# A scheduled S4D-convolution and MLP kernel: where two 64-row matmuls stand among the convolution's steps, and the settings of its order

## The chip, the cores and the metric

The kernel runs on one core of a Trainium2 chip. The metric is the device time of one execution in microseconds (us). The kernel before takes 1095.59 us (median of three runs, 1095.1 to 1095.95).

The engines are named as the profile names them: PE (TensorE, matmuls), PEld (its weight loads), DVE (VectorE), ACT (ScalarE), POOL (GpSimd) and SP (SyncE, which issues most of the DMAs).

## The reference

The output is x + s * g for 2048 tokens of 576 channels. s is a state-space convolution along the tokens (S4D: a kernel made from complex exponentials, applied by FFT), and g is a gated MLP on each token:

```python
x = A_u
xn = _layernorm(x)
s = _A_ref(xn, log_A_real, A_imag, C_real, C_imag, log_dt, D_skip)   # FFT convolution, + u * D_skip
# _B_ref: y = layernorm(xn); h = gelu(y @ w1 + b1); h @ w2 + b2      (w1: 576x4608, w2: 4608x576)
g = _silu(_B_ref(xn, w1, b1, w2, b2))
return x + s * g
```

## The kernel before, in words

**The MLP sets the frame.** The 2048 tokens go in four blocks of 512 and the 4608 hidden channels in 12 groups of 384 (three chunks of 128), which gives 48 *slots* (`NSLOT`). A slot has 11 *positions* (`NPOS`): three of layer 1 (`layer1`, line 633, tiles mxa and mxb in PSUM) and eight of layer 2 (`layer2`, line 707). Every operand is split into a high and a low part, so a product takes three matmuls. In layer 1 a chunk takes 14 matmuls of 128 rows by 512 columns: 12 for the first 512 channels, and for the last 64 channels one on `w1r` with XR (64 rows of high and 64 rows of low parts together) and one more on `w1s`. Layer 2 takes 72 matmuls of 288 columns in a slot. Behind a layer-1 chunk stand a Gelu (ACT, line 671), a copy to the high part `hh` (ACT, 674) and a subtraction for the low part `hl` (DVE, 677); behind each fourth of layer 2 stands an addition to `acc` (DVE, 717).

**The pair.** `pair` (line 616) does the `w1s` work of two chunks, 0 and 2, by two matmuls of 64 rows each, one on array rows 0 to 63 and one on rows 64 to 127, side by side. Then neither chunk needs its `w1s` matmul, and takes 13 instead of 14 (`BEGUN` holds the chunks). The second one reads a copy of XR's upper half, which `load_pair` brings to partitions 64 to 127 in a tile that the program calls bias.

**The convolution** is done in six chunks of 96 channels. Each is a row of steps on PE, between ACT and DVE work: two x1 (array tile 64x128), two k1 (32x128), four s2 (64x32), two inv (32x64), one i1 (128x64), and the tables of the kernel (kg, 128x32, 36 in all). A kg may *ride* inside another step (`ride`, `lead`); inside an x1 it stands behind the x1's matmuls, inside the others ahead of them. All steps take their PSUM from two banks-of-two named cv, which DVE or ACT must empty before the next step but one.

**The order is planned when the program is built.** The class `Order` keeps a clock for each engine. PE's list is the frame of slots; `pe_turns` is asked behind certain positions whether a step of the convolution goes in there. It takes a step if its inputs are ready by the plan's clocks by some margin, if the pace (`EDGE`) allows it, and for a kg if ALONE and DUE allow it. X1, S2, INV, I1 and KG are the plan's durations of the steps, `LEN` those of the positions. The other engines' work is put in where the plan finds room; of steps that are ready together the line of `od.line()` that stands first goes first; HOLD puts single steps one or two places later than planned. Each engine then runs its list in that order. `pe_turns` sets a pair ahead of the first convolution step at a slot's edge (position 10), if its weights and its copy are there.

Of the kernel before, what the change touches and what calls it, by code (L numbers as in the profile page):

```python
# [18 lines left out]
P = 128  # L19
# [13 lines left out]
G = 3  # L33
# [18 lines left out]
class Order:  # L52
# [44 lines left out]
    def take(self, eng, dur, ready, tbl=None):  # L97
        start = max(self.t[eng], ready)
        if eng == "DVE" and self.shared and start < self.t["POOL"] - 0.4:
            dur *= 1.1  # L100
        if tbl and tbl != self.tbl:
            dur += 1.28
            self.tbl = tbl
        self.t[eng] = start + dur
        return start + dur + self.LAT
# [119 lines left out]
def mixer_kernel(ctx, tc, u, log_a_real, a_imag, c_real, c_imag, log_dt, d_skip, w1, b1, w2, b2,  # L225
                 f1, f2, g2, g1, tvals, ident, out, parts=("mlp", "s4d")):
    nc = tc.nc
# [6 lines left out]
    def bank2(name):  # L234
        return ps.tile([P, 2, TB], F32, name=name, bufs=2 if name == "cv" else 1)
# [236 lines left out]
    XR = sb.tile([P, 2, TB], F32R, name="XR")  # L472
    XQ = {}
# [58 lines left out]
    W = {}  # L532
# [56 lines left out]
    HID, LAST, Q1, Q2, IDM = {}, {}, {}, {}, []  # L589
    turn = [0]  # L590

    def mx(i):
        return "mxa" if (turn[0] + i) % 2 == 0 else "mxb"

    BEGUN = set()
# [10 lines left out]
            XQ[0] = sb.tile([P, D], F32R, name="bias2")[:, :TB]  # L606
        nc.sync.dma_start(XQ[0][64:].bitcast(F32), XR[:64, tb].bitcast(F32))

    def pair(tb):

        Q1[0] = bank2(mx(1))
        for e, x in enumerate((XR[:64, tb], XQ[0][64:])):
            r, k = slice(64 * e, 64 * e + 64), e * (G - 1)
            nc.tensor.matmul(Q1[0][:, e], W[1][3][r, k * P:(k + 1) * P], x, start=True, stop=False,  # L616
                             skip_group_check=True)
        BEGUN.update((0, G - 1))

    def layer1(g, tb, i):  # L620
        h, lo, r1, r2 = W[1]
# [331 lines left out]
    def tables(b):  # L953
# [37 lines left out]
        def weigh(part):  # L991
# [10 lines left out]
            else:  # L1002
# [7 lines left out]
                 step("DVE", dve(SB * NV), f(phase, 0), need=[("kg", b - 2)] if b > 1 else []),  # L1010
                 step("DVE", dve(n), f(phase, 1), hold=HOLD.get(("phase", b), 0)), step("ACT", act(SB * NV), whole),
                 step("DVE", dve(SB * NV), frac, hold=HOLD.get(("frac", b), 0)), step("ACT", act(SB * NV), fold, mark=("fold", b))],
                [step("ACT", act(SB * NV), f(sin, 0), need=[("fold", b)], mark=("sin", b, 0), tbl="sin"),
# [3 lines left out]
                + [step("DVE", dve((2, 2, 1, 1)[part] * n), f(weigh, part), need=[("sin", b, 1)],  # L1017
                        mark=("wu", b) if part == 3 else None, hold=HOLD.get(("weigh", b, part), 0)) for part in range(4)])

# [33 lines left out]
    def ride(host):  # L1053

        if not kl["steps"] or kl["steps"][0]["eng"] != "PE" or host["mark"][0] == "inv":
            return
        st, out = kl["steps"][:2]
        need = st["need"]
        if any(m not in od.marks for m in need) or max([kl["ready"]] + [od.marks[m] for m in need]) > od.t["PE"] - 0.4:
            return  # L1060
        del kl["steps"][:2]
        GUEST.append(st["fn"])
        host["dur"] += KG

        def behind():
            end = od.t["PE"] + od.LAT
            od.marks[st["mark"]] = kl["ready"] = end
            od.urgent.append((end, [dict(out, cv=0)]))
        return behind


    X1, S2, INV, I1, KG = 1.5, 1.75, 2.15, 3.05, 1.03

    HOLD = {("weigh", 19, 3): 1, ("phase", 19): 1, ("frac", 18): 2, ("k", 2, 1): (2, 1), (2, 0, 24): 1, (2, 1, 24): 1, ("k1", 2, 1, 2): 1}

    def chunk(c):

# [66 lines left out]
        def x1(i):  # L1144
# [18 lines left out]
            for d0 in (0, 24):  # L1163
                c0 = 48 * i + d0
                add("DVE", 0.9, lambda d0=d0, c0=c0: nc.vector.transpose(
                    A2[:, :, 0, c0:c0 + 24].rearrange("p k d r -> p d k r"), Q[d0]), cv=-1, hold=HOLD.get((c, i, d0), 0))

# [150 lines left out]
    NPOS = G + 8  # L1318
    NSLOT = 4 * NG
    od = Order(tc, nc)  # L1320
    od.pinned = True
    el, wl2, wl, nl2, pl, pl2, nl, ml, ml2, xl, wx, c3, c2, c1, c4, kl, tl, sl, vl, gl, odl, fl = [od.line() for _ in range(22)]
    nlh, mlh, mlt = od.line(), od.line(), od.line()
    od.lines = od.lines[-3:] + od.lines[:-3]

# [76 lines left out]


    L1 = 14 * 0.2315
    LEN = [L1] * G + [3 * n * 0.132 + 0.02 for n in (4, 2, 2, 4, 3, 3, 3, 3)]

    T0 = 12.5
    for e, t in dict(PE=0.0, ACT=4.6, DVE=3.7, POOL=3.8, SP=0.0).items():
# [98 lines left out]
    def wmark(n, which):  # L1507

        per = KB + 1 + G
        a = n * per + (0 if which == 1 else KB + 1)  # L1510
        return [("w", k) for k in range(a, a + (KB + 1 if which == 1 else G))]
# [67 lines left out]


    EDGE = 0.2, 0.6
    ALONE, DUE = 20.0, (160.0, 950.0)

    def pe_turns(limit=1, any_time=False, all_lines=True, edge=None):
        for x in (nl, pl, ml) + ((c3, c1, kl) if all_lines else ()):
            n = 0
            while n < (2 if x in (c1, nl) else limit):
                h = od.head(x)
                if h is None or h[0]["eng"] != "PE" or h[1] > od.t["PE"] + (0.3 if x is nl else -0.4):
                    break  # L1590
                if x is c1:
                    now = od.t["PE"]
                    gap = (END - now) / max(pace["left"], 1)
                    if n == 0 and pace["started"] and now < pace["last"] + EDGE[edge is None] * gap and not any_time:
                        break
                    pace["started"], pace["last"] = True, now
                    pace["left"] -= 1
                if x is kl and pace["started"]:
                    b = kl["steps"][0]["mark"][1]
                    wait = ("wu", b + 1) not in od.marks or od.t["PE"] < DUE[0] + b * (DUE[1] - DUE[0]) / NB  # L1600
                    if b < NB - 1 and od.t["PE"] < h[1] + (ALONE if wait else 3.0):
                        break
                if edge is not None and not BEGUN and x in (c3, c1, kl):
                    m = wmark(edge // 2, 1) + [("xq", edge)]
                    if all(k in od.marks and od.marks[k] < od.t["PE"] - 0.3 for k in m):
                        od.unit(lambda: pair(edge % 2), 0.24)
                behind = ride(h[0]) if x in (c1, c3) else None
                od.run(x)
                if behind:
                    behind()  # L1610
                od.pin()
                od.advance(od.t["PE"])
                n += 1

    LATER = {}

    def later(slot, pos, f):
# [53 lines left out]
    for slot in range(NSLOT):  # L1671
        turn[0] = slot + 1
        od.shared = slot > 1
        g, tb = slot // 2 % NG, slot % 2
        n = slot // 2
        final = slot >= NSLOT - 2
        for pos in range(NPOS):
            if pos < G:
# [9 lines left out]
                if pos == 2:  # L1688
                    BEGUN.clear()
                    k = slot % (2 * NG)  # L1690
# [16 lines left out]
            else:  # L1707
# [13 lines left out]
                if halves:  # L1721
                    dh = terms[0][1]
                    od.marks["z", dh] = od.t["PE"] + od.LAT
                    x = od.line()
# [3 lines left out]
                if split:  # L1728
                    add = cell[0]
                    for d in range(2) if j == 0 else (terms[0][1],):  # L1730
                        m = ("acc", slot, j, d)
# [3 lines left out]
                        x = od.line()  # L1735
# [3 lines left out]
                if last and not halves:  # L1739
# [4 lines left out]
                    elif final:  # L1744
                        x = el if slot < NSLOT - 1 else od.line()
# [3 lines left out]
                    elif g == NG - 1:  # L1749
                        for d in range(2):  # L1750
                            one, two = gate_store(4 * tb + j, d)
# [6 lines left out]
            for f in LATER.get((slot, pos), ()):  # L1758
                f()
            od.advance(od.t["PE"])  # L1760
            pe_turns(edge=slot + 1 if pos == NPOS - 1 else None, all_lines=pos in (0, 1, 2, G + 1, G + 3, G + 5, NPOS - 1))
    od.force(lambda: not od.urgent and not any(x["steps"] for x in od.lines))


# [52 lines left out]
```

## Time and profile before

| | us |
|---|---|
| median of three runs | 1095.59 |
| the profiled execution | 1095.67 |
| its span, first to last instruction | 1093.9 |
| PE busy | 1087.1 (99%) |
| DVE busy | 891.9 (82%) |
| ACT busy | 727.1 (66%) |
| POOL busy | 188.4 (17%) |

Matmuls are pipelined: a matmul of 288 columns is shown as 0.29 us long, and the next one starts 0.13 us behind it. What a matmul costs is therefore read from one start to the next, not from its duration. A row of the timeline merges instructions of one line and name that follow one another: start, time to the end of the last one, engine, line, what is written and read, shapes, and their count. The rows with "64\*128" are array tiles of 64 rows and 128 columns.

### The profile page before, as it was taken

To read this page: it belongs to the slowest core of one execution; us is meant where nothing else is said; L and a number is where in the kernel's file an instruction comes from. 1 tells how busy PE (TensorE), PEld (TensorE's weight loads), DVE (VectorE), ACT (ScalarE), POOL (GpSimd) and SP (SyncE) were. 2 spreads that over 40 slices of the span, in tenths; PEclk is the share of its full clock that TensorE was granted. 3 is DMA by queue.
4 is the path that set the end of the run, shared out by engine and by line. 5 is a ranking of instruction groups with operands and counts; after the bars stand their busy time and mean duration, and the time that the engine had idled before them with its cause. 6 is when DMAs were issued, how large, how long until landed. Compare 5 with 4: busy or idle time off the path is not lost.

```text
span 1093.9 us, 27052 instructions
## 1 busy us (share of the span) xinstructions
PE 1087.1 (99%) x11445; PEld 954.0 (87%) x11445; DVE 891.9 (82%) x1302; ACT 727.1 (66%) x1113; POOL 188.4 (17%) x261
## 2 busy tenths in 40 slices
PE   9999999999999999999999999999999999999998
PEld 7989899899888898888988888888888888888897
DVE  7798667889998879889899987997969888766367
ACT  6585699778676674767767848685675757534333
POOL 4566210153020100001100000000001021101132
PEclk9999999999999999999999999999999999999999
DMA  8746764626354152355624215143142434454444
GB/s 242 225 149 152 236 235 143 179 80 157 116 160 134 44 112 67 96 110 148 161 48 118 78 56 141 34 122 87 56 126 42 144 101 132 114 170 150 137 151 103
DMA packets 139553, 138.22 MB, mean 126 GB/s; under 512 B 88952, under 2 KB 105016, under 8 KB 138856
## 3 DMA queue, kind: packets, MB, share of 16 engines
q1 hardware_dynamic: 124424, 85.05, 29.0%
q0 software_dynamic: 14528, 50.71, 14.7%
q8 instruction: 89, 1.46, 0.6%
q10 hardware_dynamic: 480, 0.74, 0.3%
q14 instruction: 32, 0.26, 0.1%
HBM read 102.17 MB, written 36.63 MB: 127 GB/s over the span
## 4 chain that ended last, share of the span: by engine, by line
PE 95%; DVE 3%; ACT 1%; SPq 1%; issue 0%; DMA 0%; POOL 0%; DVEq 0%; ACTq 0%; POOLq 0%
PE mxb L707 20%; PE mxa L707 20%; PE mxa L633 20%; PE mxb L633 20%; PE cv L1217 3%; PE cv L1042 3%; PE cv L1260 2%; PE cv L1286 2%; PE cv L1188 1%; PE cv L1157 1%; PE mxa L1348 1%; DVE acc L717 0%; PE mxa L648 0%; SPq L1089 0%; PE mxb L616 0%
## 5 line engine op out<-in xcount | busy, mean ns | idle before, releaser
L677 DVE TENSOR_TENSOR hl<-h,hh 128x512 fp32r<-128x512 f32 x144 | 98.5, 687 | 99.2 <-ACT hh L674 98.4
L707 PE MATMUL mxa<-w2h,hh 128*128 128x288 f32 x573 | 170.3, 297 | 0.0
L707 PE MATMUL mxb<-w2h,hh 128*128 128x288 f32 x573 | 170.2, 297 | 0.0
L707 PE MATMUL mxb<-w2h,hl 128*128 128x288 f32 x573 | 169.3, 295 | 0.1
L707 PE MATMUL mxa<-w2h,hl 128*128 128x288 f32 x573 | 169.1, 295 | 0.0
L707 PE MATMUL mxa<-w2l,hh 128*128 128x288 f32 x573 | 168.6, 294 | 0.0
L707 PE MATMUL mxb<-w2l,hh 128*128 128x288 f32 x573 | 168.6, 294 | 0.0
L671 ACT ACTIVATE h<-mxa,b1t 128x512 f32<-128x512 f32 x73 | 50.1, 687 | 98.3 <-PE mxa L633 95.1
L707 PEld LDWEIGHTS mxa<-w2h,hh 128*128 128x128 f32 x573 | 107.6, 188 | 5.8 <-issue 3.0
L707 PEld LDWEIGHTS mxb<-w2h,hh 128*128 128x128 f32 x573 | 107.6, 188 | 4.3 <-issue 1.4
L707 PEld LDWEIGHTS mxb<-w2l,hh 128*128 128x128 f32 x573 | 107.6, 188 | 0.8
L707 PEld LDWEIGHTS mxa<-w2l,hh 128*128 128x128 f32 x573 | 107.6, 188 | 0.6
L707 PEld LDWEIGHTS mxb<-w2h,hl 128*128 128x128 f32 x573 | 107.5, 188 | 0.3 <-DVE hl L677 0.3
L707 PEld LDWEIGHTS mxa<-w2h,hl 128*128 128x128 f32 x573 | 107.5, 188 | 0.0
L671 ACT ACTIVATE h<-mxb,b1t 128x512 f32<-128x512 f32 x71 | 48.8, 687 | 69.7 <-PE mxb L633 67.2
L674 ACT ACTIVATE hh<-h 128x512 fp32r<-128x512 f32 x144 | 90.7, 631 | 3.7
L944 POOL DMA_DIRECT2D par<-par_s x36 | 27.8, 771 | 367.8 <-DVE mg L988 325.0
L717 DVE TENSOR_TENSOR acc<-mxa,acc 128x576 f32<-128x576 f32 x87 | 65.5, 753 | 26.0 <-PE mxa L707 25.9
L717 DVE TENSOR_TENSOR acc<-mxb,acc 128x576 f32<-128x576 f32 (+1 forms) x89 | 65.9, 741 | 17.8 <-PE mxb L707 17.7
L633 PE MATMUL mxa<-XH,w1h 128*128 128x512 f32 x284 | 79.2, 401 | 0.0
L633 PE MATMUL mxb<-XH,w1h 128*128 128x512 f32 x280 | 77.7, 399 | 0.0
L633 PE MATMUL mxa<-XL,w1h 128*128 128x512 f32 x284 | 76.1, 390 | 0.0
(277 smaller groups left out, 2494.4 us busy)
## 6 DMA issues: line engine op xcount, KB each, us to landing
raw<-in_B_w_dram SPq DMA_DIRECT2D x72, 288.0 KB, 3.4
raw<-in_B_w_dram SPq DMA_DIRECT2D x96, 192.0 KB, 3.5
par_s<-A POOLq DMA_DIRECT2D x4, 2160.0 KB, 8.1
par<-par_s POOLq DMA_DIRECT2D x36, 240.0 KB, 3.6
f2t<-f2q SPq DMA_DIRECT2D x24, 256.0 KB, 3.6
g2t<-g2p SPq DMA_DIRECT2D x24, 256.0 KB, 4.1
bias<-XR SPq DMA_DIRECT2D x42, 128.0 KB, 3.6
raw<-in_B_w_dram SPq DMA_DIRECT2D x48, 96.0 KB, 3.7
```

The lines of the kernel that those rows point to most:

```text
L633: nc.tensor.matmul(q, a, b, start=j == 0 and i not in BEGUN, stop=j == len(ops) - 1, skip_group_check=True)
L671: nc.scalar.activation(t, q, AF.Gelu_apprx_tanh, bias=b1t[:, k:k + 1], scale=1.0)
L674: LAST[0] = nc.scalar.activation(hh[:, i], t, AF.Copy)
L677: nc.vector.tensor_sub(hl[:, i], t, hh[:, i].bitcast(F32))
L707: nc.tensor.matmul(q[:, dh, :288], a[:, i, c], b[:, i, d], start=i == 0 and k == 0 and alone != 1, stop=i == G - 1 and k == 2, skip_group_ ...
L717: nc.vector.tensor_add(o, q[:, dh:dh + n, :288], b)
L944: nc.gpsimd.dma_start(PAR[b].rearrange("p (g i) k -> p g (i k)", g=4), dram(par_s, (b // 3 * 48 + b % 3 * 4) * NPAR, [[D * NPAR, P], [12 * ...
L1042: nc.tensor.matmul(q[32 * g:32 * g + 32, i // 2, i % 2 * 64:i % 2 * 64 + 64], U[:, ri, 4 * g + i, :], v[:, ri, 4 * g + i, :], start=ri == ...
L1157: nc.tensor.matmul(Q[24 * v][:, e], FP[0][r, f, 0], x[r, 12 * e:12 * e + 12], start=n == 0, stop=n == 2, skip_group_check=True)
L1217: nc.tensor.matmul(Q[i][32 * q:32 * q + 32, f, ri::2], m[r, 4 * i + q, 32 * ri:32 * ri + 32], A2[r, 4 * p + 2 * i + q // 2, :, :, q % 2], ...
L1260: nc.tensor.matmul(QI[q // 2][64 * f:64 * f + 64, q % 2, i], MAT["g2t", p + i // 2][r, i % 2, f, ri], YS[p + i // 2][0][r, i % 2, ri, f], ...
L1286: nc.tensor.matmul(Q[h][64 * y:64 * y + 64, t], g1t.rearrange("p a e -> p (a e)"), A2[:, k:k + 2, 1].rearrange("p i d r -> p i r d"), star ...
```

## The change

Four things change.

1. `pair` has a second argument i, the chunk that goes with chunk 2: 0 at a slot's edge, as before, or 1 behind position 0 of a slot, "within layer 1".
2. In `pe_turns` the pair goes behind the convolution step where that step is an x1 without a rider (`after`), and ahead of it in all other cases, as before. Within layer 1 it is set only behind such an x1.
3. Convolution steps may stand behind five positions of a slot (`TURNS`: 0, 1, 4, 6, 10) instead of seven (also 2 and 8), and with a margin of 0.1 instead of 0.4 us by the plan's clocks.
4. The plan's settings: durations of x1, s2 and inv, ALONE and DUE, HOLD (one entry in place of eight), the order of the lines, the factor by which the plan slows DVE while POOL is at work (1.05 in place of 1.1).

```diff
-    def pair(tb):
-        Q1[0] = bank2(mx(1))
-        for e, x in enumerate((XR[:64, tb], XQ[0][64:])):
-            r, k = slice(64 * e, 64 * e + 64), e * (G - 1)
-            nc.tensor.matmul(Q1[0][:, e], W[1][3][r, k * P:(k + 1) * P], x, start=True, stop=False,
+    def pair(tb, i):
+        Q1[i] = bank2(mx(1))
+        for e, k, q, x in ((0, i, Q1[i][:, 0], XR[:64, tb]), (1, 2, Q1[0][:, 1], XQ[0][64:])):
+            nc.tensor.matmul(q, W[1][3][64 * e:64 * e + 64, k * P:(k + 1) * P], x, start=True, stop=False,
...
-        BEGUN.update((0, G - 1))
+        BEGUN.update((i, 2))
...
-            dur *= 1.1
+            dur *= 1.05
...
-    X1, S2, INV, I1, KG = 1.5, 1.75, 2.15, 3.05, 1.03
+    X1, S2, INV, I1, KG = 1.55, 1.68, 2.34, 3.05, 1.03
...
+    HOLD = {(5, 1, 0): 1}
...
-    ALONE, DUE = 20.0, (160.0, 950.0)
+    ALONE, DUE = 27.3, (182.0, 862.0)
...
-                if h is None or h[0]["eng"] != "PE" or h[1] > od.t["PE"] + (0.3 if x is nl else -0.4):
+                if h is None or h[0]["eng"] != "PE" or h[1] > od.t["PE"] + (0.3 if x is nl else -0.1):
...
-                        od.unit(lambda: pair(edge % 2), 0.24)
+                after = x is c1 and h[0]["mark"][0] == "x1" and not behind
+                if two and edge is not None and not after:
+                    od.unit(lambda: pair(edge % 2, 0), 0.39)
                 od.run(x)
...
+                if two and after:
+                    od.unit(lambda: pair(slot % 2, int(edge is None)), 0.2)
...
+    TURNS = 0, 1, G + 1, G + 3, NPOS - 1,
...
-            pe_turns(edge=slot + 1 if pos == NPOS - 1 else None, all_lines=pos in (0, 1, 2, G + 1, G + 3, G + 5, NPOS - 1))
+            pe_turns(edge=slot + 1 if pos == NPOS - 1 else None, all_lines=pos in TURNS,
+                     inner=slot if pos == 0 else None)
```

In the order that comes out of it there are 18 pairs in place of 16. Before, 5 stand ahead of an x1 and 11 ahead of another step; now 4 stand ahead of an x1 (with a rider), 2 behind an x1, and 12 ahead of another step. None stands within layer 1. Leaving the pairs aside, PE has the same 102 convolution steps (a kg with its host counted as two), and they stand in 74 groups between MLP matmuls before and now. The last i1 moves from the middle of a slot's layer 2 to the edge ahead of that layer.

The first pair, on PE at the edge of the 13th slot, before (616 is the pair, 1157 the x1, 707 layer 2, 633 layer 1):

```order
1070 L707 MATMUL mxa<-w2l,hh 128x288
1071 L707 MATMUL mxa<-w2h,hl 128x288
1072 L616 MATMUL mxb<-XR,w1s 128x512
1073 L616 MATMUL mxb<-bias_773,w1s 128x512
1074 L1157 MATMUL cv<-pr,f2t 128x384 x4
1075 L1157 MATMUL cv<-ys,f2t 128x384 x4
1076 L1157 MATMUL cv<-pr,f2t 128x384 x4
1077 L633 MATMUL mxb<-XH,w1h 128x512 x4
```

The same edge on PE now (the changed file's lines are two lower):

```order
1070 L705 MATMUL mxa<-w2l,hh 128x288
1071 L705 MATMUL mxa<-w2h,hl 128x288
1072 L1155 MATMUL cv<-pr,f2t 128x384 x4
1073 L1155 MATMUL cv<-ys,f2t 128x384 x4
1074 L1155 MATMUL cv<-pr,f2t 128x384 x4
1075 L614 MATMUL mxb<-XR,w1s 128x512
1076 L614 MATMUL mxb<-bias_773,w1s 128x512
1077 L631 MATMUL mxb<-XH,w1h 128x512 x4
```

The pair has moved behind the x1's twelve matmuls, and layer 1 follows it directly.

The last i1 on PE before (1286 is the i1), within layer 2:

```order
4031 L707 MATMUL mxb<-w2l,hh 128x288
4032 L707 MATMUL mxb<-w2h,hl 128x288
4033 L1286 MATMUL cv<-A_83,g1t 64x384 x8
4034 L707 MATMUL mxa<-w2h,hh 128x288
4035 L707 MATMUL mxa<-w2l,hh 128x288
```

And now, at a slot's edge, on PE:

```order
3999 L705 MATMUL mxa<-w2h,hl 128x288
4000 L614 MATMUL mxb<-XR,w1s 128x512
4001 L614 MATMUL mxb<-bias_7170,w1s 128x512
4002 L1284 MATMUL cv<-A_83,g1t 64x384 x8
4003 L631 MATMUL mxb<-XH,w1h 128x512 x4
4004 L631 MATMUL mxb<-XL,w1h 128x512 x4
4005 L631 MATMUL mxb<-XH,w1l 128x512 x4
4006 L631 MATMUL mxb<-XR,w1r 128x512
```

The step has a pair ahead of it now, and the chunk of layer 1 behind it has 13 matmuls.

DVE between the first and the second s2 of the third convolution chunk, before (1234 multiplies out of cv and so empties it, 1240 sums, 677 is hl, 717 the addition to acc, 963 to 1003 make tables):

```order
655 L1234 TENSOR_TENSOR pr<-cv,kk 128x768
656 L1240 TENSOR_TENSOR ys<-pr 128x2x2x96
657 L966 TENSOR_TENSOR w<-w,par 128x16x32
658 L677 TENSOR_TENSOR hl<-h_7037,hh 128x512
659 L1003 SCALAR_TENSOR_TENSOR w<-w,mg 128x16x32
660 L1234 TENSOR_TENSOR pr<-cv,kk 128x768
```

DVE at the same two s2 now:

```order
635 L675 TENSOR_TENSOR hl<-h_6814,hh 128x512
636 L583 TENSOR_TENSOR w1l<-raw,w1h 128x384 x4
637 L583 TENSOR_TENSOR w1s<-raw,w1r 128x384
638 L961 TENSOR_TENSOR w<-par,tv 128x16x65
639 L964 TENSOR_TENSOR w<-w,par 128x16x32
640 L715 TENSOR_TENSOR acc<-mxb,bias_6330 128x576
641 L1232 TENSOR_TENSOR pr<-cv,kk 128x768
642 L715 TENSOR_TENSOR acc<-mxa,bias_6330 128x576
643 L1238 TENSOR_TENSOR ys<-pr 128x2x2x96
644 L970 TENSOR_TENSOR w<-w 128x16x65
645 L715 TENSOR_TENSOR acc<-mxb,bias_6330 128x576
646 L1232 TENSOR_TENSOR pr<-cv,kk 128x768
```

The two multiplications stood in a slot's layer 1 before and stand in its layer 2 now: additions to acc stand between them, which wait for layer 2, and five weight splits and two table steps ahead of them.

## Rows read from the trace of the kernel before

**Rows 1.** The page: its first line, and PE in the table of engines.

```profile
span 1093.9 us, 27052 instructions
PE 1087.1 (99%) x11445; PEld 954.0 (87%) x11445; DVE 891.9 (82%) x1302; ACT 727.1 (66%) x1113; POOL 188.4 (17%) x261
```

**Rows 2.** Busy time by stretch; columns: stretch, its length, PE, PEld, DVE, ACT, POOL, clock.

```profile
13.00:250.00 237.00, 237.00 (x1706) 214.79 (x1706) 185.88 (x311) 179.77 (x319) 96.46 (x114) 1.00 0.59 180
250.00:560.00 310.00, 310.00 (x3524) 269.34 (x3527) 273.42 (x378) 220.75 (x312) 29.53 (x45) 1.00 0.43 113
560.00:800.00 240.00, 239.91 (x3081) 208.30 (x3071) 213.22 (x285) 164.36 (x232) 14.38 (x18) 1.00 0.31 87
800.00:1030.00 230.00, 230.00 (x2754) 198.89 (x2754) 174.20 (x247) 131.35 (x196) 28.21 (x48) 1.00 0.42 119
```

**Rows 3.** Timeline of PE in a layer 2, at its longest wait.

```profile
567.07 0.29 PE L707 MATMUL mxa<-w2l,hh 128*128 128x288 f32 x1
...
567.86 0.29 PE L707 MATMUL mxb<-w2l,hh 128*128 128x288 f32 x1
568.24 0.40 PE L707 MATMUL mxb<-w2h,hl 128*128 128x288 f32 x1
568.48 0.29 PE L707 MATMUL mxb<-w2h,hh 128*128 128x288 f32 x1
```

**Rows 4.** Timeline of PE: the end of a layer-1 chunk, then a kg.

```profile
578.58 1.07 PE L633 MATMUL mxb<-XH,w1l 128*128 128x512 f32 x4
579.49 0.39 PE L633 MATMUL mxb<-XR,w1r 128*128 128x512 f32 x1
579.72 0.39 PE L633 MATMUL mxb<-XR,w1s 128*128 128x512 f32 x1
580.03 0.58 PE L1042 MATMUL cv<-w 128*32 128x64 f32 x25
```

**Rows 5.** Timeline of PE: layer 2, a pair, an s2.

```profile
296.11 0.29 PE L707 MATMUL mxa<-w2h,hl 128*128 128x288 f32 x1
...
296.33 0.50 PE L616 MATMUL mxb<-bias,w1s 64*128 64x512 f32 x1
296.76 1.60 PE L1217 MATMUL cv<-A,f2t 64*32 64x192 f32 x64
```

**Rows 6.** Timeline of PE: layer 2, a pair, an x1, layer 1.

```profile
250.22 0.29 PE L707 MATMUL mxa<-w2h,hl 128*128 128x288 f32 x1
...
250.44 0.50 PE L616 MATMUL mxb<-bias,w1s 64*128 64x512 f32 x1
250.78 0.52 PE L1157 MATMUL cv<-pr,f2t 64*128 64x384 f32 x4
...
251.48 0.51 PE L1157 MATMUL cv<-pr,f2t 64*128 64x384 f32 x4
251.93 0.73 PE L633 MATMUL mxb<-XH,w1h 128*128 128x512 f32 x2
```

**Rows 7.** Timeline of PE: layer 2, an x1 without a pair, layer 2.

```profile
549.33 0.29 PE L707 MATMUL mxa<-w2h,hl 128*128 128x288 f32 x1
549.54 0.62 PE L1157 MATMUL cv<-pr,f2t 64*128 64x384 f32 x4
...
550.80 0.40 PE L707 MATMUL mxb<-w2h,hh 128*128 128x288 f32 x1
```

**Rows 8.** Timeline of DVE around two s2 of the third chunk.

```profile
578.65 0.75 DVE L717 TENSOR_TENSOR acc<-mxa,bias 128x576 f32<-128x576 f32 x1
579.32 0.68 DVE L988 TENSOR_TENSOR mg<-par 128x512 f32<-128x512 f32 x1
...
585.40 1.24 DVE L963 TENSOR_TENSOR w<-par,tv 128x1040 f32<-128x1040 f32 x1
586.55 0.95 DVE L1234 TENSOR_TENSOR pr<-cv,kk 128x768 f32<-128x768 f32 x1
587.54 0.56 DVE L1240 TENSOR_TENSOR ys<-pr 128x384 f32<-128x384 f32 x1
```

More of the change, by code (lines that the diff above doesn't have):

```diff
@@ L1069, in ride @@
         return behind
-    X1, S2, INV, I1, KG = 1.5, 1.75, 2.15, 3.05, 1.03
-    HOLD = {("weigh", 19, 3): 1, ("phase", 19): 1, ("frac", 18): 2, ("k", 2, 1): (2, 1), (2, 0, 24): 1, (2, 1, 24): 1, ("k1", 2, 1, 2): 1}
+    X1, S2, INV, I1, KG = 1.55, 1.68, 2.34, 3.05, 1.03
+    HOLD = {(5, 1, 0): 1}
     def chunk(c):
@@ L1321, in mixer_kernel @@
     od.pinned = True
-    el, wl2, wl, nl2, pl, pl2, nl, ml, ml2, xl, wx, c3, c2, c1, c4, kl, tl, sl, vl, gl, odl, fl = [od.line() for _ in range(22)]
+    el, wl2, wl, nl2, pl, pl2, nl, ml, ml2, xl, wx, c3, c1, c2, kl, c4, sl, tl, vl, gl, odl, fl = [od.line() for _ in range(22)]
     nlh, mlh, mlt = od.line(), od.line(), od.line()
@@ L1404, in mixer_kernel @@
     L1 = 14 * 0.2315
-    LEN = [L1] * G + [3 * n * 0.132 + 0.02 for n in (4, 2, 2, 4, 3, 3, 3, 3)]
+    LEN = [L1] * G + [3 * n * 0.1319 + 0.02 for n in (4, 2, 2, 4, 3, 3, 3, 3)]
     T0 = 12.5
@@ L1581, in mixer_kernel, with pe_turns @@
     EDGE = 0.2, 0.6
-    ALONE, DUE = 20.0, (160.0, 950.0)
-    def pe_turns(limit=1, any_time=False, all_lines=True, edge=None):
+    ALONE, DUE = 27.3, (182.0, 862.0)
+    def pe_turns(limit=1, any_time=False, all_lines=True, edge=None, inner=None):
         for x in (nl, pl, ml) + ((c3, c1, kl) if all_lines else ()):
@@ L1602, in pe_turns @@
                         break
-                if edge is not None and not BEGUN and x in (c3, c1, kl):
-                    m = wmark(edge // 2, 1) + [("xq", edge)]
-                    if all(k in od.marks and od.marks[k] < od.t["PE"] - 0.3 for k in m):
-                        od.unit(lambda: pair(edge % 2), 0.24)
+                slot = edge if edge is not None else inner
+                two = slot is not None and not BEGUN and x in (c3, c1, kl) and all(
+                    k in od.marks and od.marks[k] < od.t["PE"] - 0.3 for k in wmark(slot // 2, 1) + [("xq", slot)])
                 behind = ride(h[0]) if x in (c1, c3) else None
+                after = x is c1 and h[0]["mark"][0] == "x1" and not behind
+                if two and edge is not None and not after:
+                    od.unit(lambda: pair(edge % 2, 0), 0.39)
                 od.run(x)
```

## The prediction

> **What bounds the kernel now.** I read the page first, then busy time by stretch, then PE's timeline. On the page [rows 1] PE is busy 1087.1 of 1093.9 us, and DVE, the next, 82%. The remaining 6.8 us of PE lie at the two ends: from 13 to 1030 us PE lacks 0.09 us in all [rows 2]. The granted clock is 1.00 throughout, the 2.4 GHz level. So the time is the number of matmuls times what each takes, unless "busy" hides waits, which it can do: a matmul that waits behind a pipelined one counts as busy.
>
> The timeline settles that, read from one start to the next. Layer 2's rhythm: six intervals from 567.07 to 567.86, 0.79 / 6 = 0.132 us each. Behind it the next two starts are 0.38 and 0.24 apart [rows 3], 0.25 and 0.11 over the rhythm: the longest wait inside the kernel, with PE counted busy through it. I went through all of PE's intervals so, against others of the same kind (same tile, same size, same neighbours). Nine are more than 0.04 us longer than their kind, 0.92 us together, and these two are the first and the second of them. PE waits for 0.9 us of 1095.7. The DVE, ACT and DMA work, however it is ordered, lies beside PE; only the sum of PE's intervals and new waits can move the time.
>
> **Part 1, where the pairs stand.** PE executes as many matmuls as before: a pair of two takes the place of two. What differs is the price of a pair by its neighbours.
> - A 512-column matmul of layer 1 costs 0.91 / 4 = 0.2275 (578.58 to 579.49, [rows 4]); two of them, which a pair replaces, 0.455.
> - Ahead of an s2: pair at 296.33, s2 at 296.76 [rows 5], so 0.43. The step has its switch of array tile with or without the pair (its neighbours are 128*128 on both sides), so this is the whole price. Gain 0.455 - 0.43 = 0.025.
> - Ahead of an x1, which has the pair's tile, 64*128: pair 250.44, x1 250.78, layer 1 251.93 [rows 6]. The pair takes 0.34 and the x1 1.15. Without a pair the x1 takes 549.54 to 550.80 [rows 7], 1.26 (1.25 at most other places): the pair pays the switch that the x1 else pays, so it costs 0.34 - 0.10 = 0.24. Gain 0.215.
> - Behind an x1: no row shows it. Bounds: below, the pair's own pitch with nothing at its end, 0.35 / 2 = 0.175 per matmul (its 384-column neighbours in the x1 go four in 251.48 to 251.93, under it); above, the 0.43 ahead of an s2. In between: the pair's first matmul takes the place of the x1's exit (0.27 becomes 0.175), and its last has an exit of 512 columns into another tile, which is what 579.72 to 580.03 shows [rows 4], 0.31. So 0.175 + 0.31 - 0.27 = 0.215. I take this, as it is made of three rows of like shapes; gain 0.24.
>
> Before, 5 pairs stand ahead of an x1 and 11 ahead of another step: 5 x 0.215 + 11 x 0.025 = 1.35. Now 4 stand ahead of an x1, 2 behind one and 12 ahead of another step: 4 x 0.215 + 2 x 0.24 + 12 x 0.025 = 1.64. The change gains **0.29 us**. With the bounds of a pair behind an x1 (0.175 to 0.43: gain 0.28 to 0.025) it is 0.37 to a loss of 0.14. None of it can be measured: about 0.2%, 2.2 us, is what a measurement of this kernel can tell from no change.
>
> The heading of the change, a pair within layer 1, doesn't occur in the order at all: that branch wants an x1 without a rider behind position 0, and none falls there. Its cost is nothing because it isn't there.
>
> **Part 2, five places instead of seven, and a smaller margin.** The 102 convolution steps stand in 74 groups between MLP matmuls before and now, so the switches between 128*128 and the small tiles are as many. The steps' inner matmuls are the same. Cost of the places alone: zero. What moves is when steps run: middle chunks come some 30 to 40 us earlier in the list, the last i1 one half slot. Of every step moved, DVE's and ACT's work, its table loads and its DMAs move along. SP's queue has the same issues, and the last i1 and all behind it stay ahead of the last slots' layer 2, so the end of the kernel (the 6.8 us at the ends) keeps its work; I cost it at zero. What covers it: the last block's MLP, whose DVE share past 800 us is 174.2 of 230 [rows 2].
>
> The margin is a matter of waits. Before, steps went in only if their inputs were ready 0.4 us ahead by the plan's clocks; now 0.1. PE has run behind its inputs on almost all conv steps, so this cover can be thinner by 0.3 without being used up. Queued behind a step that does wait is all of PE, each 0.1 us lost there is lost at the end. Nothing in the trace of before has that thinner cover; its price is bounded by 0 (all steps in time) and, for a step late by its DVE work, by that work: 0.75 for an addition, 0.95 for the multiplication [rows 8].
>
> **Part 3, the settings.** These order DVE, ACT and POOL. DVE has the most to lose: in 560 to 800 us it is busy 213.2 of 240 [rows 2]. Its work isn't more, and its share in a slot stays near 0.9. Cost: zero if no result is late on PE.
>
> **Sum.** 1095.67 (profiled execution; 0.08 above the median of 1095.59) - 0.29 = 1095.4.
>
> **Rivals.**
> *New waits behind DVE (slower).* The place is the two s2 of the third chunk. Before, DVE's work between them had no addition to acc; now two additions stand between and around the two multiplications, and additions wait for layer 2's last matmuls. cv must be emptied by the multiplication before PE's second next step can write it. Working: from the first addition's input (24th of 72 layer-2 matmuls) to the kg that rides ahead of the second s2 PE needs 48 x 0.132 = 6.3, less about 0.3 for the exit ahead of the kg: about 6.1 us. DVE has in it three additions, two multiplications, the sums and one table step: 3 x 0.75 + 2 x 0.95 + 0.56 + 1.24 = 5.95 [rows 8]; back to back less, as 0.75 shows 0.67 from start to start (578.65 to 579.32), about 5.5. Ahead of these stand five weight splits and a table step, about 4.7 us against some 4.0 until the first addition's input comes; so DVE begins 0.25 to 0.7 late. 5.5 + 0.7 is 0.1 more than 6.1; 5.95 + 0.7 is 0.55 more; 5.5 + 0.25 is 0.35 less. The point from which it decides: DVE being later than 0.15 to 0.6 us at its first addition is a wait of PE. Such a kg ahead of an s2 stands at 15 places now (14 before). If a third of them, five, wait 0.5, that is 2.5 us: 1095.4 + 2.5 = 1097.9, slower by just over 0.2%. For it: DVE's 0.89 busy in this stretch and the smaller margin. Against: before, with DVE as full, the nine waits were 0.92 us together, and layer 2 gives DVE a run of matmuls in which it catches up.
>
> *The old waits go.* The plan is new and its waits are too; if it had none, 1095.4 - 0.9 = 1094.5. For: the waits of before stood at special places [rows 3]. Against: the smaller margin makes more of them, not fewer.
>
> *A pair is worth its full half everywhere.* If a switch of array tile took nothing, every pair would save one 512-column matmul wherever it stands, and two more pairs would save 2 x 0.2275 = 0.455: 1095.2. Against it: the pair ahead of the s2 takes 0.43 where two full matmuls take 0.455 [rows 4, 5].
> The Trainium skill, "TensorEngine Tiling (Array Packing)", section Theoretical Speedup, gives up to 2x for a contraction of at most 64 rows; by that rule alone this rival is the forecast. The trace doesn't agree away from an x1 (0.025 of 0.2275 saved) and nearly does beside one (0.215).
>
> *The change doesn't do what it says.* No pair within layer 1, and the two behind an x1 give back what they gain (upper bound, 0.43): 1095.67 + 0.14 = 1095.8. The same to any measurement.
>
> **How the numbers follow.** Forecast, the sum of PE's intervals with waits as before within some tenths: 0.62, 1095.4 (1094.9 to 1096.5). Old waits gone, 1094.5: 0.10. Full half, 1095.2: 0.04. Nothing gained, 1095.8: 0.06. Together 0.82, all within 0.2% but for a few hundredths. DVE's waits: 0.16, about 1098, of which one in five stays under the 2.2 us and some goes to 1100. Something that no row offers, faster by over 2.2 us: 0.02. For such a gain PE's sum would have to fall by 2.2, and all the pairs together, 18, save 1.64. So faster 0.02, same 0.83, slower 0.15. The range reaches from under the waits-gone case, 1094.3, to the middle of the slower one, 1098.2; it leaves out about 1 in 10.
>
> **What the changed profile would show.** PE busy near 1086.8, still 99%, and at most 0.1 us idle in the stretches from 13 to 1030. A pair behind an x1: last x1 matmuls to pair without a gap, pair to layer 1's next matmul at 0.175 + 0.31. Pairs ahead of an s2 at 0.43. If DVE's waits come, intervals at a kg or s2 in a slot's layer 2 between 0.2 and 1 us longer than their kind, with DVE's multiplication as what they wait for, from the third chunk on. The forecast is wrong if these add up to over 2 us, or if layer 2's rhythm isn't 0.132 any more. The prediction would be wrong below if intervals of layer 1 or 2 became shorter, which no term here allows.

## The result, and the profile of the changed kernel

| | before | changed |
|---|---|---|
| median, us | 1095.28 | 1097.18 |
| lowest to highest, 22 runs each | 1094.75 to 1096.02 | 1096.53 to 1098.82 |
| span of the profiled execution | 1093.9 | 1095.3 |
| last start of a matmul in it | 1088.56 | 1089.92 |

The changed kernel takes 1.0019 times as long, with a 95% interval of 1.0013 to 1.0025: slower by 1.9 us, where 0.3 us less was forecast. It is within the 0.2% that the prediction called no change, but its sign is clear: the fastest of 22 runs of the changed kernel is slower than the slowest of 22 of the other. Its runs also scatter more, over 2.3 us instead of 1.3.

The page of the changed kernel, its first line, the engines, and the first line of the chain of work that ended last:

```profile
span 1095.3 us, 27055 instructions
...
PE 1086.3 (99%) x11445; PEld 952.1 (87%) x11445; DVE 890.1 (81%) x1302; ACT 723.4 (66%) x1109; POOL 188.0 (17%) x261
...
PE 95%; DVE 2%; DMA 1%; ACT 1%; SPq 0%; issue 0%; ACTq 0%; DVEq 0%
```

PE is busy 0.8 us less than before [rows 1], and yet the span is 1.4 us longer: PE has new idle time. A hundredth of the chain is DMA now. Busy time by stretch tells where (columns as in [rows 2]: stretch, length, PE, PEld, DVE, ACT, POOL, clock, DMA share, GB/s):

```profile
13.00:250.00 237.00, 236.81 (x1702) 214.50 (x1702) 185.96 (x313) 181.25 (x319) 100.84 (x122) 1.00 0.59 181
250.00:560.00 310.00, 308.42 (x3597) 268.27 (x3596) 278.25 (x385) 220.93 (x313) 25.63 (x39) 1.00 0.43 114
560.00:800.00 240.00, 240.00 (x3064) 208.21 (x3063) 213.39 (x286) 168.55 (x234) 13.10 (x17) 1.00 0.32 88
800.00:1030.00 230.00, 230.00 (x2678) 197.97 (x2677) 166.42 (x238) 121.31 (x188) 29.71 (x50) 1.00 0.45 128
```

All of the new idle time lies ahead of 560 us: 1.58 us in the second stretch, 0.19 in the first. From 560 on there is none, and the third chunk, where the prediction feared DVE, is undisturbed. PE's waits by what ended them (total us, times, longest; left out are three rows of the kernel's first 13 us):

```profile
PE mxb L631 <- ACT h L669: 1.6, 1, 1.6
...
PE mxa L705 <- DVE hl L675: 0.2, 1, 0.2
```

One matmul of layer 1 waits 1.6 us for a Gelu, once. PE's timeline there: it is the 13th slot, whose edge the order rows of the change show, with the pair now behind the first x1.

```profile
250.88 0.61 PE L1155 MATMUL cv<-pr,f2t 64*128 64x384 f32 x4
...
252.03 0.39 PE L614 MATMUL mxb<-bias,w1s 64*128 64x512 f32 x1
252.36 1.19 PE L631 MATMUL mxb<-XH,w1h 128*128 128x512 f32 x4
...
258.38 0.39 PE L631 MATMUL mxa<-XR,w1s 128*128 128x512 f32 x1
260.35 1.20 PE L631 MATMUL mxb<-XH,w1h 128*128 128x512 f32 x4 [1.58 <-ACT h L669]
```

The first chunk of layer 1 begins at 252.36, the second ends with the matmul at 258.38, and the third begins at 260.35 instead of 258.61 (258.38 + 0.23): 1.74 us late. Its releaser is the Gelu of the first chunk, which reads the same PSUM tile, mxb. ACT's timeline tells why that Gelu is late:

```profile
252.87 1.07 ACT L967 ACTIVATE w<-w 128x1040 int32<-128x1040 f32 x1
256.18 2.11 ACT L1122 ACTIVATE xt<-xc 128x768 f32<-128x768 f32 x1 [2.24 <-DMA xc<-xn_s]
258.31 1.28 ACT L669 ACT_TABLE_LOAD   x1
259.61 0.69 ACT L669 ACTIVATE h<-mxb,b1t 128x512 f32<-128x512 f32 x1
```

ACT has stood still for 2.24 us, with the Gelu behind the head of its list. At the head is `xt`, a copy that turns the second half of the first convolution chunk's input, and that waits for its load, xc. In the kernel before ACT does the three Gelus first:

```profile
256.41 0.69 ACT L671 ACTIVATE h<-mxb,b1t 128x512 f32<-128x512 f32 x1
...
262.59 2.10 ACT L1124 ACTIVATE xt<-xc 128x768 f32<-128x768 f32 x1
```

There `xt` begins at 262.59, long after its load has landed. In the changed kernel the load itself is slower, too. SP issues it from 246.96 on, and POOL issues three loads of u_s (288 KB each) meanwhile:

```profile
246.96 5.35 SPq L1087 DMA_DIRECT2D xc<-xn_s  x4
```

```profile
248.32 1.79 POOL L358 DMA_DIRECT2D u_s<-in_A_u_dram  x3
```

The four DMAs of xc take from issue to landing, at least, in the middle and at most, first in the changed kernel, then in the one before:

```profile
DMA to landing us min/median/max: 5.6/6.6/7.7
```

```profile
DMA to landing us min/median/max: 4.0/4.9/5.8
```

The second new wait is at 65.5 us. On DVE, a second half of BATCH_NORM_STATS stands ahead of the subtraction hl, which layer 2 needs:

```profile
64.32 0.82 DVE L423 BATCH_NORM_STATS2 st<-w 128x6 f32<-128x288 f32 x2
...
65.30 0.64 DVE L675 TENSOR_TENSOR hl<-h,hh 128x512 fp32r<-128x512 f32 x1
```

On PE it shows as two starts 0.48 apart, 0.35 over the rhythm (the next start is 0.10 over it):

```profile
65.52 0.29 PE L705 MATMUL mxa<-w2l,hh 128*128 128x288 f32 x1
66.00 0.40 PE L705 MATMUL mxa<-w2h,hl 128*128 128x288 f32 x1 [0.19 <-DVE hl L675]
```

**The sum.** Added up over PE's intervals as in the prediction, everything behind 13 us that is more than 0.04 us over its kind is 0.78 us before and 2.90 now, of which 1.85 at 258.4 and 0.45 at 65.5. That is +2.12. (Another 0.45 lies at 22.2 to 23.1 us, where layer 2 waits for hl; the traces of e1, e2, e10 and e11 below have no such wait there, so it comes and goes between executions. Against it, the waits of before at 482 and 567 us [rows 3] are gone, about 0.5.) The intervals at their normal length sum to 0.31 us less (the pairs; 0.29 was forecast). The first layer-1 matmul came 0.33 us earlier in this execution (12.40 instead of 12.73; the order up to there is the same). 2.12 - 0.31 - 0.33 = 1.48; the last matmul's start moved by 1.36, and the 0.12 between them is left open.

### The profile page after: what moved, and what is told of

It reads as the page before. It is cut to its first block, busy times and chain, and to the rows that moved or that the text cites. A ratio compares the mean times of both kernels' runs of the same rounds, so it can differ in the third digit from the quotient of the medians.

```text
span 1095.3 us, 27055 instructions
## 1 busy us (share of the span) xinstructions
PE 1086.3 (99%) x11445; PEld 952.1 (87%) x11445; DVE 890.1 (81%) x1302; ACT 723.4 (66%) x1109; POOL 188.0 (17%) x261
## 4 chain that ended last, share of the span: by engine, by line
PE 95%; DVE 2%; DMA 1%; ACT 1%; SPq 0%; issue 0%; ACTq 0%; DVEq 0%
PE mxb L705 20%; PE mxa L705 20%; PE mxa L631 20%; PE mxb L631 20%; PE cv L1040 3%; PE cv L1215 3%; PE cv L1258 2%; PE cv L1284 2%; PE cv L1186 1%; PE cv L1155 1%; DMA xc<-xn_s 1%; DMA acc<-in_A_u_dram 0%; PE mxa L646 0%; PE mxa L614 0%; PE cv L516 0%; DVE A L807 0%
## 5 line engine op out<-in xcount | busy, mean ns | idle before, releaser
L715 DVE TENSOR_TENSOR acc<-mxa,acc 128x576 f32<-128x576 f32 x87 | 65.5, 753 | 23.3 <-PE mxa L705 22.8
```

The source lines that it names most:

```text
L715: nc.vector.tensor_add(o, q[:, dh:dh + n, :288], b)
```

## Theories

- **A.** One step on ACT does it: xt, ahead of a Gelu, waits for a load that has become slower; PE waits for the Gelu. The rest of the loss is the step on DVE at 64.3 us.
- **B.** The change's own parts cost it: the pairs behind an x1 (the pair may tie the third chunk to the Gelu of the first), or the thinner margin and the fewer places.
- **C.** The prediction's rival: DVE makes PE wait, from the third chunk on.

## Experiments on the changed kernel, with one step moved

The program's plan was left as it was in these, so that only the named instructions move. "Before" is the kernel before, measured beside them on the same chip.

| kernel | median, us | before, us | ratio, 95% interval |
|---|---|---|---|
| e1: xt behind the Gelu | 1095.42 | 1095.02 | 1.0006 (0.9997 to 1.0015) |
| e2: u_s loads later | 1095.50 | 1095.02 | 1.0005 (0.9996 to 1.0013) |
| e3: xt twice | 1101.48 | 1095.02 | 1.0055 (1.0041 to 1.0068) |
| e6: xt behind the Gelu, statistics behind hl | 1094.92 | 1095.02 | 1.0000 (0.9991 to 1.0009) |
| e12: e6 again | 1095.02 | 1095.50 | 0.9997 (0.9988 to 1.0005) |
| e9: the two pairs ahead of their x1 | 1097.29 | 1095.50 | 1.0017 (1.0008 to 1.0026) |
| e11: no pair in the 13th slot | 1097.39 | 1095.50 | 1.0017 (1.0009 to 1.0026) |
| e10: e6 without any pair | 1096.50 | 1095.50 | 1.0007 (0.9998 to 1.0016) |

**xt behind the Gelu (e1).** `hold` issues a step so many places later on its engine, without telling the plan. The copy pr, which reads xt, goes behind the Gelu with it.

```diff
-    HOLD = {(5, 1, 0): 1}
+    HOLD = {(5, 1, 0): 1, ("t", 0, 1): 2, ("x", 0, 1): (1, 0)}
...
-                four.append(step("ACT", act(2000), turn, need=need))
+                four.append(step("ACT", act(2000), turn, need=need, hold=HOLD.get(("t", c, i), 0)))
```

> The changed kernel with one thing put back: the copy xt<-xc of the first convolution chunk's second half, and the pr behind it, stand on ACT behind the first Gelu and its copy hh, not ahead of them. All other engines' rows are as in the changed kernel. Theory A (one step on ACT: xt waits for its DMA, the Gelu of a layer-1 chunk is queued behind it, and PE behind the Gelu): the wait of 1.7 us at 258.4 us goes, 1095.3 us (1094.9 to 1095.6), PE idle under 0.3 us between 13 and 560 us. Theory B (the pairs that moved behind an x1, or the smaller margin, cost it in many places): nothing of this is undone, 1097.2. Theory C (DVE-made waits from the third chunk on, the prediction's rival): 1097.2.

Measured 1095.42, in A's range. ACT's timeline now has the Gelu where PE has it ready, and nothing waits for the load:

```profile
255.95 0.69 ACT L669 ACTIVATE h<-mxb,b1t 128x512 f32<-128x512 f32 x1 [0.38 <-PE mxb L631]
...
257.21 2.10 ACT L1122 ACTIVATE xt<-xc 128x768 f32<-128x768 f32 x1
```

The wait for the Gelu is gone from PE's list. B and C, by which nothing should have changed, are wrong by 1.8 us. It says that xt's place decides, not yet why its load is late.

**The u_s loads later (e2).**

```diff
-        gl["steps"].append(step("POOL", 0.7, lambda b=b: order_u(b)))
+        gl["steps"].append(step("POOL", 0.7, lambda b=b: order_u(b), hold=int(b < 3)))
```

> The changed kernel with three DMAs of POOL (u_s<-in_A_u, 288 KB each, issued at 248.3 to 250.1 us, while xc is being loaded) put behind POOL's next DMA, some 23 us later. ACT, DVE, PE and SP keep their order, xt stays ahead of the Gelu. Theory A with contention as the reason of the late landing: xc lands 6 to 7 us after its first issue as in the kernel before, not 9; xt begins 2 us sooner and the wait at 258.4 shrinks to 0 to 0.4: 1095.3 to 1095.8. Theory A with another reason for the late landing (SP's own issue, the weight loads): landing stays at 9 us, 1097.2. Theories B and C: 1097.2.

Measured 1095.50. Here xt stays ahead of the Gelu; only the load is quicker. Its four DMAs, and ACT's timeline:

```profile
DMA to landing us min/median/max: 3.9/5.6/5.8
```

```profile
253.71 2.11 ACT L1122 ACTIVATE xt<-xc 128x768 f32<-128x768 f32 x1 [0.45 <-DMA xc<-xn_s]
...
257.13 0.69 ACT L669 ACTIVATE h<-mxb,b1t 128x512 f32<-128x512 f32 x1
```

The longest landing is back at 5.8 us, ACT's wait is 0.45 instead of 2.24, and the Gelu ends at 257.8, ahead of PE's third chunk. SP's four issues take as long as in the changed kernel (5.26 us against 5.35; 3.73 before), so it is the landing that the u_s loads slow. So both conditions are needed: xt ahead of the Gelu, and the load slowed by the transfers beside it. Either one alone costs nothing measurable. From the first issue of xc to the start of xt 7.4 us pass here, and 8.7 to 9.5 in the five traces where xt waits with three u_s loads beside it (the changed kernel, e3, e7, e9, e11).

**xt twice (e3).**

```diff
-                nc.scalar.activation(T["x"], get(), AF.Copy)
+                for _ in range(1 + ((c, i) == (0, 1))):
+                    nc.scalar.activation(T["x"], get(), AF.Copy)
```

> The changed kernel with the copy xt<-xc of the first chunk's second half done twice, one behind the other, both ahead of the Gelu: the suspected delay is made larger by the 2.0 to 2.1 us of one such copy. Theory A: the wait at 258.4 grows from 1.7 to 3.8 us, 1099.2 (1098.8 to 1099.6). Theories B and C, for which ACT has room there: 1097.2 to 1097.5.

Measured 1101.48: 4.3 us over the changed kernel where A expected 2.0. The direction is A's, the size is not. PE's timeline:

```profile
262.32 2.07 PE L631 MATMUL mxb<-XH,w1h 128*128 128x512 f32 x4 [3.24 <-ACT h L669]
...
267.61 0.55 PE L631 MATMUL mxb<-XR,w1r 128*128 128x512 f32 x1
```

The wait grew from 1.58 to 3.24, 1.7 us, nearly as A says (2.1; xt could begin 0.2 us sooner). But the third chunk behind it takes 5.29 us to its last matmul (262.32 to 267.61) where it takes 2.85 in the changed kernel (260.35 to 263.20): 2.4 us more. The granted clock tells why (columns as before, the clock is third from the end; a value between 0.50 and 1.00 is a stretch with both levels in it):

```profile
255.00:259.10 4.10, 4.08 (x19) 3.04 (x17) 4.10 (x5) 3.05 (x2) 0.00 (x0) 1.00 0.84 262
259.10:262.30 3.20, 0.00 (x0) 0.00 (x0) 0.72 (x2) 3.17 (x4) 0.00 (x0) 0.81 0.36 52
262.30:264.00 1.70, 1.68 (x4) 1.39 (x5) 0.96 (x2) 1.70 (x3) 0.00 (x0) 0.50 0.99 115
264.00:267.20 3.20, 3.20 (x9) 2.42 (x9) 1.97 (x4) 0.73 (x2) 0.00 (x0) 0.50 0.18 23
```

While PE stood idle the clock fell to 0.50, the 1.2 GHz level, and it stayed there over the third chunk: 1.7 us of wait and 2.4 us of slow matmuls make 4.1 of the 4.3 us.

**Statistics behind hl as well (e6, and e12).** To e1's edit comes one hold more:

```diff
-                                        hold=int((b0, t, i) in ((8, 1, 0), (8, 2, 1), (8, 3, 0)))))
+                                        hold={(8, 1, 0): 1, (8, 2, 1): 1, (8, 3, 0): 1, (12, 2, 1): 1}.get((b0, t, i), 0)))
```

> As the first of these, and the second half of one BATCH_NORM_STATS on DVE at 64.3 us is put behind the subtraction hl, where it stood before the change. Theory A with the rest of the loss at 65.5 us (a wait of 0.35 and 0.10 behind it for hl): 0.3 to 0.45 us faster than the first of these, 1094.9 (1094.5 to 1095.2), so under the kernel before by the 0.3 us that the pairs were worth in the prediction. Theories B and C: 1096.8 to 1097.2.

> The kernel with xt and the statistics put back once more, on the chip of these runs, as what the kernel without pairs is compared with: 1094.9 (1094.5 to 1095.3) by theory A.

Measured 1094.92 and 1095.02; e6 is 0.5 us under e1, beside which it was measured. PE's list of waits in e6, the whole of it, has only rows of the first 13 us:

```profile
PE mxa L1346 <- POOL XL L1339: 1.3, 1, 1.3
PE mxa L646 <- ACT XH L520: 0.4, 1, 0.4
```

So two steps on two in-order engines account for all of the loss. By its time the version is no faster than the kernel before (1.0000 and 0.9997, both intervals include 1): what the new order gains is too small to see there. In the traces it shows: from the first matmul of layer 1 to the last matmul of all there are 1075.83 us in the kernel before, 1077.52 in the changed one, 1075.24 in e6 and 1075.41 in e12, one execution each.

**The two pairs ahead of their x1 (e9).** The pair is issued ahead of the x1, and the plan's clock still takes it behind.

```diff
+                if two and after:
+                    pair(slot % 2, int(edge is None))
                 od.run(x)
...
-                    od.unit(lambda: pair(slot % 2, int(edge is None)), 0.2)
+                    od.unit(lambda: None, 0.2)
```

> The changed kernel with the two pairs that stand behind an x1 issued ahead of that x1, and no other instruction of any engine in another place (the plan is left as it was). Theory A: nothing of the wait goes, x1 and pair together take the same 1.48 to 1.49 us either way: 1097.0 to 1097.5. Theory B (the pair behind the x1 is what costs it): 1095.3.

Measured 1097.29: the place of the pair is not the cause. Its timeline gives the price of a pair ahead of the same x1:

```profile
251.03 0.50 PE L614 MATMUL mxb<-bias,w1s 64*128 64x512 f32 x1
...
252.51 1.20 PE L631 MATMUL mxb<-XH,w1h 128*128 128x512 f32 x4
...
260.82 1.19 PE L631 MATMUL mxb<-XH,w1h 128*128 128x512 f32 x4 [1.88 <-ACT h L669]
```

Pair and x1 take 1.48 us (251.03 to 252.51), as they do in the changed kernel with the pair behind (250.88 to 252.36). In this execution, the slowest of its eleven (1099.5), the wait was 1.88 us, and the clock fell again, with PE already at work (1.00 until 262, then 0.59 in the 2 us shown and 0.78 in the 4 us that follow):

```profile
262.00:264.00 2.00, 2.00 (x8) 1.54 (x7) 1.80 (x5) 1.22 (x3) 0.00 (x0) 0.59 0.78 97
```

**No pair in the 13th slot (e11).** Of the 18 pairs the first is left out; the two chunks take their w1s matmuls.

```diff
+    NPAIR = []
...
     def pair(tb, i):
+        BEGUN.update((i, 2))
+        NPAIR.append(1)
+        if len(NPAIR) == 1:
+            return
+        REAL.update((i, 2))
...
```

(`layer1` asks REAL instead of BEGUN.)

> The changed kernel without the one pair of the 13th slot, whose third chunk has the wait: its first and third chunk take 14 matmuls, no other instruction moves. If the third chunk's first matmul waits for the Gelu of the first in any case (they share a PSUM tile), PE comes 0.0 to 0.2 us later to it and the wait stays at 1.5 to 1.7 us: 1097.0 to 1097.5. If the pair makes the tie, PE goes through the third chunk and waits, if at all, in layer 2: 1095.3 to 1096.3.

Measured 1097.39, and the wait on PE, whose lines are seven higher here, is still there:

```profile
PE mxb L638 <- ACT h L676: 1.5, 1, 1.5
```

The third chunk waits for the Gelu of the first with a pair or without. In the program both are halves of one PSUM tile, which would explain it; no run here tests that. B is out in this form too.

**Without any pair (e10).** As e11, with the return for all 18, on e6.

> The kernel with xt and the statistics put back, without any of its 18 pairs: each of the 36 chunks takes its own matmul on w1s again, and no other instruction moves. It measures the prediction's prices of the pairs together: by these (4 x 0.215 + 2 x 0.24 + 12 x 0.025) PE's sum grows by 1.64 us, so 1.2 to 1.7 us over the kernel with them in the same call, about 1096.5. By the rival 'a pair is worth its full half everywhere' it grows by 18 x 0.2275 = 4.1 us, about 1099.

Measured 1096.50 where e12, the same kernel with the pairs, has 1095.02: 1.48 us for the 18 pairs, against 1.64 by the prediction's prices and 4.1 by the rival of the full half. It is not exact: e12's eleven runs lie between 1094.49 and 1096.43, and e10's trace has one x1 0.3 us late (at 925.05, behind its input ys), which e12's has not. The full half is out all the same. The Trainium skill, "TensorEngine Tiling (Array Packing)", section Theoretical Speedup, gives up to 2x for a contraction of at most 64 rows; the run agrees only with the "up to": 1.48 of 4.1 us arrive, near what the prices by neighbours say.

## Experiments in which the plan was made anew

| kernel | median, us | before, us | ratio, 95% interval |
|---|---|---|---|
| e4: changed kernel, pairs always ahead | 1101.28 | 1094.90 | 1.0059 (1.0046 to 1.0072) |
| e5: changed kernel, 1.1 | 1105.51 | 1094.90 | 1.0098 (1.0084 to 1.0111) |
| e7: kernel before, 1.05 and the new HOLD | 1110.12 | 1094.90 | 1.0133 (1.0117 to 1.0148) |
| e8: kernel before, the new HOLD | 1096.31 | 1094.90 | 1.0013 (1.0004 to 1.0022) |

Here one setting is put back (in e4 with the plan's duration of a pair, in e7 with HOLD), and the whole order follows from it. The edits:

```diff
# e4, in pe_turns
-                after = x is c1 and h[0]["mark"][0] == "x1" and not behind
+                after = False
...
-                    od.unit(lambda: pair(edge % 2, 0), 0.39)
+                    od.unit(lambda: pair(edge % 2, 0), 0.24)
# e5
-            dur *= 1.05
+            dur *= 1.1
# e7 (from the kernel before)
-            dur *= 1.1
+            dur *= 1.05
# e7 and e8 (from the kernel before): HOLD of the changed kernel
```

> The changed kernel with the pairs ahead of the convolution step everywhere, as before the change; settings, places and margin stay. In the order that comes out xt still stands ahead of the Gelu in the 13th slot, and three u_s loads have become two there. Theory A: the wait at the third layer-1 chunk of that slot stays, 1.2 to 1.8 us, and the pairs give back under 0.1 us: 1096.5 to 1097.4. Theory B in its form 'the pair behind the x1 ties the third chunk to the Gelu of the first': the wait goes, 1095.3.

> The changed kernel with one number put back: 1.1 in place of 1.05, by which the plan slows DVE while POOL is at work. In the order that comes out, xt stands behind all three Gelus and the statistics behind hl, as in the kernel before; pairs, places, margin, durations, ALONE, DUE, HOLD are the changed ones. Theory A with this number as the one that moved xt: 1094.9 (1094.5 to 1095.3), no wait over 0.2 us at 258 or 65 us. Theory B (another part of the change costs it): 1096.5 to 1097.2.

> The kernel before with 1.05 in place of 1.1 and the changed kernel's HOLD (with the old list of held steps the order can't be made), nothing else of the change: no moved pair, seven places, margin 0.4, old durations. In its order xt stands ahead of the Gelu in the 13th slot. Theory A: the wait comes here too, 1096.9 to 1097.4. Theories B and C: 1095.0 to 1095.6, as the next kernel.

> The kernel before with the changed kernel's HOLD alone, so what the one above has besides 1.05. xt stands behind the three Gelus. Theory A: as the kernel before or a little over it, since seven held steps are given up: 1095.0 to 1095.6. Theory B with HOLD as the culprit: 1096.9.

All four missed what was expected, e8 by 0.6 us and the others by 4 to 13 us, and waits on PE are behind much of it. The longest behind the first 13 us, of e7, of e5 and of e4:

```profile
PE mxb L707 <- DVE hl L677: 3.0, 1, 3.0
...
PE mxb L633 <- ACT h L671: 1.6, 1, 1.6
```

```profile
PE mxb L705 <- DVE hl L675: 2.4, 3, 1.0
```

```profile
PE mxb L705 <- DVE hl L675: 3.2, 1, 3.2
...
PE mxb L631 <- ACT h L669: 0.7, 1, 0.7
```

On the disputed wait they are clear. e7 and e8 differ in the number 1.05 alone, and e8 has no such wait at 258 us. e7 has none of the moved pairs, the fewer places or the smaller margin, and has the wait of 1.6 us for the Gelu; its timeline is the changed kernel's to 0.05 us:

```profile
258.36 0.39 PE L633 MATMUL mxa<-XR,w1s 128*128 128x512 f32 x1
260.30 1.19 PE L633 MATMUL mxb<-XH,w1h 128*128 128x512 f32 x4 [1.56 <-ACT h L671]
```

e5 has all the pairs, the places and the margin, and no wait for a Gelu. So the number 1.05, by which the plan believes DVE to be less slowed by POOL, is what brought xt ahead of the Gelu (and the statistics ahead of hl: at 65.5 us e7 has the 0.35 us as well, e5 doesn't). e4 adds a middle case, though in another plan: two u_s loads stand beside xc instead of three, and 8.35 us pass from the first issue to xt. ACT waits 1.38 us instead of 2.24, and PE's third chunk is 0.85 us late instead of 1.74.

```profile
255.52 2.12 ACT L1122 ACTIVATE xt<-xc 128x768 f32<-128x768 f32 x1 [1.38 <-DMA xc<-xn_s]
```

What A had wrong is that putting the number back would give the time back. Each new plan has waits of its own at other places: in e4 at 479.65 one of 3.4 us, and it is the same mechanism on DVE, two turns (STREAM_TRANSPOSE) that wait for their DMAs with hl behind them:

```profile
479.34 0.71 DVE L491 STREAM_TRANSPOSE row<-row 128x512 f32<-128x512 f32 x1 [2.24 <-DMA row<-y_s]
481.38 0.71 DVE L491 STREAM_TRANSPOSE row<-row 128x512 f32<-128x512 f32 x1 [1.32 <-DMA row<-y_s]
...
482.45 0.68 DVE L675 TENSOR_TENSOR hl<-h,hh 128x512 fp32r<-128x512 f32 x1
```

In e5 and e7 the work behind the last matmul grew too, from 5.3 us (1088.56 to 1093.9) to 8.9 and 9.7; why is left open. e8 came nearest: HOLD alone costs 1.4 us, in two waits of 0.7 us at 567.0 and 568.9, so the entries that the change gave up (seven; the section on the change says eight) were worth having in the old plan; from 560 us on the changed one has no wait without them.

## Why the prediction was wrong

- **What bounds the kernel: right.** The time is PE's intervals and its waits; nothing else moved the end.
- **Part 1, the pairs: right.** Forecast gain 0.29 us, in the intervals 0.31. A pair behind an x1 costs 1.48 - 1.25 = 0.23, between the 0.215 taken and the 0.24 ahead of one; its place is worth nothing. All 18 pairs: 1.64 by the prices, 1.48 measured (e10 and e12, to some tenths). That no pair stands within layer 1 was so. The working of the 0.215 was not right, though: it lets the pair's two matmuls follow one another, 0.175 and then 0.31, and the traces of both kernels have them start side by side (at 250.44 before, at 252.03 now), with layer 1 0.33 us behind them in the changed kernel where 0.485 was forecast. That the sum came out is luck in part.
- **Part 2, places and margin: right as far as tested.** From 560 us on there is no idle time at all. Both waits of the changed kernel came from another setting (e7 and e5). The rival by which the old waits go came true in part: of 0.9 us about 0.5 is gone.
- **Part 3, the settings: the step that failed.** "Cost: zero if no result is late on PE", with DVE named as the engine that has the most to lose. The condition was left unchecked for ACT, where the Gelu stood behind xt and xt behind a load slowed by other loads, and for DVE at 65 us. The term measured 1.85 us at 258.4 and 0.45 at 65.5, where zero was put; against them stood 0.3 us of gain. DVE's busy share, on which I argued, is beside the point: at 256 us ACT was idle, not busy, behind a load.
- **"Of every step moved, DVE's and ACT's work, its table loads and its DMAs move along"** was written and not followed up. The order of the changed kernel showed xt ahead of a Gelu; that is a step with a DMA as input ahead of one that PE needs, and should have had a row and a price. Even so the price would have come out near nothing with the landing of before: xt's first half ends at 244.8 + 2.1 = 246.9, where SP's issues for the second begin; with the 7.1 us of load of the kernel before (first issue 245.23, last issue at 248.38 and 4.0 more) xt would have begun at 254.0 and the Gelu ended at 254.0 + 2.1 + 1.3 + 0.7 = 258.1, half a microsecond ahead of PE. What was missing besides is what else is loaded meanwhile: the u_s loads stand 5 us earlier on POOL (248.32; before at 253.30). So a wait of 0 to 2 us was there to be foreseen as a rival, not as a certainty.
- **The slower rival had the wrong engine and place.** It gave 1097.9 by DVE at the third chunk; nothing of it came. That 1097.18 lies near it is chance.

## What to carry to other kernels

When a change reorders in-order engines, go through each list for steps that wait for a DMA and now stand ahead of one that the bounding engine waits for, and price them by the load's own landing and by what else is loaded at that time; the engine's busy share says nothing about it. The plan's fixed price of a load (5.0 us here, 9.0 from first issue to last landing in the changed kernel) is where such an order goes wrong. To test which part of a reordering costs, move the single instruction and keep the plan: putting back one setting made another plan, here 1.4 to 15 us slower than the kernel before (e8 and e7 at the two ends), with waits in other places.

## What the runs showed of the hardware

A wait of PE can cost more than itself. Behind 3.24 us of idle time (e3) the granted clock was 0.50 for some 5 us, and 512-column matmuls started 0.43 us apart instead of 0.2275; e9's 1.88 us was followed by 0.59 and 0.78, and e7's 3.03 us at 482 by 0.50 (486 to 488). Length alone doesn't decide it: behind 1.58 us in the changed kernel the clock stayed 1.00, and so it did in e4 behind 3.25 us:

```profile
483.18 0.40 PE L705 MATMUL mxb<-w2h,hl 128*128 128x288 f32 x1 [3.25 <-DVE hl L675]
```

```profile
483.18:485.00 1.82, 1.82 (x13) 1.82 (x14) 1.82 (x4) 1.63 (x2) 0.00 (x0) 1.00 0.06 9
```

What decides stays open. It is not why the changed kernel scatters over 2.3 us where the one before scatters over 1.3: the mean granted clock of each of its 22 executions is 0.999 or 1.000, and its slowest, 1098.82, has 1.000, while the profiled executions of e9 and e3, with their falls, have 0.997 and 0.996. The landing of the load would be a reason for the scatter; no run here tests it.
